# The first loads of an attention and MoE kernel: batch 0's first k as fp32 over SyncE's queue, its last fifth of v over the casting queue

## The chip, the cores and the metric

The kernel runs on one core of a Trainium2 chip. The metric is the device time of one execution in microseconds (us). TensorE is called PE in the profile, VectorE DVE, ScalarE ACT, GpSimd POOL and SyncE SP.

## The reference

Inputs are q, k and v of 8 batches, 8 heads, 576 positions and 64 dimensions, and two weight matrices, all fp32. Each head's output is the sum of two attentions. The first works on means over 4 neighbouring positions (144 of them) and is repeated 4 times; the second is local, over positions less than 4 apart. The heads are then put side by side (4608 tokens of 512 features), and a feed-forward block follows.

```
out_up    = repeat(attention(mean4(q), mean4(k), mean4(v)), 4)
out_local = attention(q, k, v) where |i - j| < 4
x   = (out_up + out_local), heads side by side      # 4608 x 512
h   = x @ w_in                                      # 4608 x 2048
out = (h * sigmoid(1.702 * h)) @ w_out              # 4608 x 512
```

## The kernel before

The tokens are worked through in 9 groups of 512. For each group `mm1` multiplies by w_in (L738) and `mm2` by w_out (L808), and the attention of the next batch is threaded between these matmuls. Only batch 0's attention has no matmuls to lie beside: it is the prologue, written out by hand from L847 to L938, and the order of the program's lines is the order on each engine (a manual schedule).

Data come in through two kinds of queue. A DMA issued by GpSimd casts fp32 to bf16 on its way (`load_1` for k and q, `load_vb` for values, `load_w_in`, `load_w_out`); one issued by SyncE or ScalarE moves bytes as they are. GpSimd's DMAs share eight semaphores in turn, so that each waits for the landing of the one issued eight before it.

The prologue's loads come in this order. At L847 `load_v` takes values chunk 4 of 5 (the last fifth) as fp32 in two halves of 128 KB, one over SyncE's queue and one over ScalarE's; ScalarE casts it into the bf16 tile vb at L865 (`prep_v`, recorded at L325). GpSimd issues k and q of heads 0 to 3, k and q of heads 4 to 7 (288 KB each as bf16), then chunks 0 to 3 of the values by `load_vb`, two halves of 64 KB each, then the first quarter of w_in. Between these loads GpSimd makes index tables (`iota_mask`, `iota_psel`), from which VectorE makes an identity, the mask bar `off` and the steps `rv` (`make_off`, `make_ident`, `make_psel`) and a bias (`make_bias`), and ScalarE a selection matrix psel (`end_psel`: seven Abs at L166, a Relu at L169, two Exp at L171).

VectorE transposes each k and q tile in 32x32 blocks (`prep_1`, L261) and sums groups of four positions (`reduce_qk`, L304). TensorE computes local scores (`scores`: the bar at L381, the products at L394) and, before them, throwaway matmuls from `warm` (L606). ScalarE exponentiates (L477, L483). `prep_vd_pe` (L362) sums four neighbouring values by matmuls with psel, first from chunks 0 and 1, then from 1, 2 and 3; its second call takes chunks 3 and 4. After the first call come the products with the values (`av_local0`, L499, all five chunks; `av_down0`, L513 and L522), a normalisation on VectorE (L541 to L549), the transposes back (L564, L575) and the first matmuls with w_in.

The persistent tile xT (four tiles of 128 x 4608 bf16) receives the attention's result, one batch after another; the last of the four gets batch 0's columns at L591, late in the prologue, and later batches' columns after that.

Of the kernel before, what the change touches and what calls it, by code (L numbers as in the profile page):

```python
# [8 lines left out]
FP32 = mybir.dt.float32  # L9
BF16 = mybir.dt.bfloat16  # L10
# [9 lines left out]
def kernel(  # L20
# [9 lines left out]
    nc = tc.nc  # L30
    B, H, S, D = q.shape
    SD = S // 4
    HP = H // 2
# [16 lines left out]
    ldp = ctx.enter_context(tc.tile_pool(name="loads", bufs=1))  # L50
# [10 lines left out]
    xT = [persist.tile([128, B * S], BF16, name=f"xT{i}") for i in range(HP)]  # L61
# [11 lines left out]
    def pm_tile():  # L73
        turn["m"] += 1
        return PM[turn["m"] % 2]
# [10 lines left out]
    di = consts.tile([128, 128], FP32, name="di")  # L86
    dr = consts.tile([128, 1], FP32, name="dr")
    bias = consts.tile([128, 4], FP32, name="bias")
# [5 lines left out]
    def iota_psel():  # L94
        for par in range(2):
            sl, c = halves[par], 2 * KSTART[par] - 512 * par - 3
            nc.gpsimd.iota(db[sl, 0:3], pattern=[[-72, 3]], base=c + 144,
                           channel_multiplier=-6, **it)
            nc.gpsimd.iota(db[sl, 3:7], pattern=[[72, 2], [-384, 2]], base=c + 228,
                           channel_multiplier=-6, **it)  # L100
# [8 lines left out]
    def fill():  # L109
        nc.vector.memset(wz, 0.0)  # L110
        nc.vector.memset(wf, 0.0)
        for t in kdT:
            nc.vector.memset(t[:, SD:160, :], 0.0)
        for t in vbs:
            nc.vector.memset(t[:, :, :, 64:65], 1.0)
        for t in vds:
            nc.vector.memset(t[:, :, :, 64:65], 4.0)
        for t in es:
            nc.vector.memset(t[:, :, 300:304], 1.0)
        for t in eds:  # L120
            nc.vector.memset(t[:, :, 432:480], 1.0)


    def make_off():
        nc.vector.tensor_tensor(out=dm, in0=dm, in1=dm, op=ALU.mult)
        nc.vector.tensor_single_scalar(out=dm, in_=dm, scalar=9.5, op=ALU.is_lt)
        nc.vector.tensor_scalar(
            out=off, in0=dm, scalar1=-1.0, scalar2=1e6, op0=ALU.add, op1=ALU.mult
        )
# [7 lines left out]
    def make_ident(di):  # L137
        nc.vector.tensor_single_scalar(out=id128, in_=di, scalar=0.0, op=ALU.is_equal)

    def make_bias():  # L140
        nc.vector.memset(bias[:, 3:4], -3.0)
        nc.vector.tensor_copy(out=bias[:, 0:2], in_=rv)
        nc.vector.tensor_scalar(
            out=bias[:, 0:2], in0=bias[:, 0:2], scalar1=-1.0, scalar2=400.0,
            op0=ALU.add, op1=ALU.mult,
        )

    rv = consts.tile([128, 2], FP32, name="rv")
    r2 = consts.tile([128, 2], FP32, name="r2")

    def make_psel():
        nc.vector.tensor_single_scalar(
            out=rv, in_=dr.to_broadcast([128, 2]), scalar=57.5, op=ALU.is_lt
        )
        nc.vector.tensor_single_scalar(
            out=r2, in_=dr.to_broadcast([128, 2]), scalar=65.5, op=ALU.is_gt
        )
        nc.vector.scalar_tensor_tensor(
            out=r2[:, 0:1], in0=dr, scalar=121.5, in1=r2[:, 0:1],
            op0=ALU.is_lt, op1=ALU.mult,  # L160
        )
        nc.vector.tensor_tensor(out=rv, in0=rv, in1=r2, op=ALU.add)

    def end_psel():
        for m in range(7):
            nc.scalar.activation(  # L166
                out=dp[:, m], in_=di[:, 0:64], func=AF.Abs, scale=8.0, bias=db[:, m : m + 1]
            )
        nc.scalar.activation(out=dp, in_=dp, func=AF.Relu, bias=bias[:, 3:4])  # L169
        for sl, c in ((slice(0, 1), 1), (slice(1, 7), 0)):  # L170
            nc.scalar.activation(  # L171
                out=psel[:, sl], in_=dp[:, sl],
                func=AF.Exp, scale=-400.0, bias=bias[:, c : c + 1],
            )


    qf, kf, vf = {}, {}, {}

    def load_1(name, src, store, b, qd):
        t = ldp.tile(  # L180
            [128, 1152], BF16, name=f"{name}b{qd}", tag=f"{name}b{qd}", bufs=2
        )
        nc.gpsimd.dma_start(  # L183
            out=t,
            in_=bass.AP(
                tensor=src.tensor, offset=src[b, 4 * qd].offset,
                ap=[[1152, 128], [1, 1152]],
            ),
        )
        store[b, qd] = t  # L190

    def load_qk(b, qd):
        load_1("k", k, kf, b, qd)
        load_1("q", q, qf, b, qd)

    def load_v(b, gate=None, chunks=range(5), queues=(nc.sync, nc.sync)):
        t = ldp.tile([128, 5, H, D], FP32, name="vf", tag="vf")
        vf[b] = t
        if gate is not None:
            gate(t[0:1, 0, 0, 0:1])  # L200
        for i in chunks:
            for par in range(2):
                queues[par].dma_start(
                    out=t[64 * par : 64 * par + 64, i],
                    in_=bass.AP(
                        tensor=v.tensor,
                        offset=v[b, 0].offset + (114 * i + KSTART[par]) * D,
                        ap=[[D, 64], [S * D, H], [1, D]],
                    ),
                )  # L210

    def load_vb(b, i):
        for par in range(2):
            nc.gpsimd.dma_start(
                out=vbs[b % 2][64 * par : 64 * par + 64, i, :, 0:D],
                in_=bass.AP(
                    tensor=v.tensor,
                    offset=v[b, 0].offset + (114 * i + KSTART[par]) * D,
                    ap=[[D, 64], [S * D, H], [1, D]],
                ),  # L220
            )
# [35 lines left out]
    def prep_1(name, b, qd):  # L257
        store, dst = {"k": (kf, kT), "q": (qf, qT)}[name]
        tt = work.tile([128, S, 2], BF16, name=f"{name}T{qd}", tag=f"{name}T{qd}", bufs=1)
        t32 = tt.rearrange("p t a -> p (t a)").bitcast(FP32)  # L260
        nc.vector.transpose(  # L261
            out=t32.rearrange("p (i c) -> p c i", c=18),
            in_=store[b, qd].bitcast(FP32).rearrange("p (c d) -> p c d", c=18),
        )
        dst[b, qd] = tt
# [57 lines left out]
    def prep_v(b, eng, i=slice(0, 5), h=slice(0, H)):  # L323
        cp = eng.copy if eng is nc.scalar else eng.tensor_copy
        cp(out=vbs[b % 2][:, i, h, 0:D], in_=vf[b][:, i, h])  # L325
# [277 lines left out]
    def warm(n, cols=512, t=None, z=wz):  # L603
        t = pm_tile() if t is None else t
        for _ in range(n):
            nc.tensor.matmul(  # L606
                t[:, 0:cols], lhsT=z[:, 0:128], rhs=z[:, 0:cols], start=True, stop=True
            )
# [233 lines left out]
    o, y, x = {}, {}, {}  # L842

    def after(src, eng):
        return lambda t: eng.tensor_copy(out=t, in_=src)

    load_v(0, chunks=[4], queues=(nc.sync, nc.scalar))  # L847
    nc.scalar.preload_act_table_set("exp_and_others")
    load_qk(0, 0)
    load_1("k", k, kf, 0, 1)  # L850
    iota_mask()
    load_1("q", q, qf, 0, 1)
    iota_psel()
    fill()
    for i in range(4):
        load_vb(0, i)
    load_w_in(0, 512)
    warm(3, z=wf)
    warm(5, 256)
    make_off()  # L860
    make_ident(di)
    make_psel()
    make_bias()
    end_psel()
    prep_v(0, nc.scalar, 4)  # L865
    prep_1("k", 0, 0)
    prep_1("q", 0, 0)
    sp = scores(0, 0, PA[0:2])
# [9 lines left out]
    for qd in range(NQ):  # L878
        load_qk(1, qd)
# [60 lines left out]
    for g in range(n_groups):  # L940
        b = g + 1
        if g == 0:
# [13 lines left out]
            for qd in range(NQ):  # L956
                load_qk(2, qd)
            nc.gpsimd.memset(v4[32:64], 0.0)
            for x, c in ((0, 1.0), (1, 4.0)):
                nc.vector.memset(ones[:, x, :], c)  # L960
            load_v(2, gate=after(w_out_bf[0:1, 14, 0:1], nc.gpsimd))
            load_v4(2)
        elif b == 2:
# [11 lines left out]
            load_qk(b + 1, 0)  # L975
            prep_vx(b)
            load_v(b + 1)
            prep_v4(b, nc.gpsimd, (0,))
            pool_qk(b, 1, "q")
# [77 lines left out]
```

## Time and profile before

| what | before |
|---|---|
| median of 3 runs | 309.1 us (309.04 to 310.23) |
| profiled execution | 308.58 us |
| its span, first to last instruction | 306.8 us |
| granted TensorE clock | 0.999 |
| busy: PE, DVE, ACT, POOL | 298.0, 187.1, 212.9, 178.9 us |
| share of the chain that ended last: PE, DMA, issue | 93%, 4%, 1% |

The span is the time between the first and last instruction of the profiled execution; its whole time holds 1.78 us more. Times in the trace count from the span's start. A busy PE is not one at its peak, since matmuls overlap. The chain that ended last is followed back from the last instruction, at each step to what released it, or to the instruction before it on its engine.

### The profile page before, as it was taken

The numbers are of one execution on the slowest core, as the hardware profiler recorded it, in microseconds if no ns is written. First come the engines' busy times: TensorE is split into PE (matmuls) and PEld (weight loads), VectorE is DVE, ScalarE is ACT, GpSimd is POOL, SyncE is SP. The second block draws the span as 40 slices with busy tenths as digits, with TensorE's granted clock in tenths as the row PEclk, the third lists the DMA queues.
The fourth block names the chain that finished last, engine by engine and source line by source line (L and its number), as shares of the span: only waits on it lengthen the run. The fifth ranks groups of instructions, "written<-read, shape, count | busy, mean of one in ns | idle before, by whom it ended". The sixth has DMA issues, their size and how long they took to land.

```text
span 306.8 us, 8494 instructions
## 1 busy us (share of the span) xinstructions
PE 298.0 (97%) x3551; PEld 147.8 (48%) x3551; DVE 187.1 (61%) x354; ACT 212.9 (69%) x351; POOL 178.9 (58%) x217
## 2 busy tenths in 40 slices
PE   7879999999999999999999999999999999999995
PEld 3455455444554455445544554455444544444444
DVE  6865523966999689886897689777975430000000
ACT  5545887867887788668966896689769876226511
POOL 8855792599698968976797669845983300000000
PEclk9999999999999999999999999999999999999999
DMA  7999999999899969826973598425101110010012
GB/s 147 152 203 209 173 132 213 177 221 215 177 230 188 188 133 226 219 46 113 232 211 66 88 218 232 84 77 150 72 0 37 36 71 0 34 71 34 0 68 71
DMA packets 64662, 40.01 MB, mean 130 GB/s; under 512 B 44656, under 2 KB 56048, under 8 KB 64624
## 3 DMA queue, kind: packets, MB, share of 16 engines
q0 software_dynamic: 18352, 14.81, 35.8%
q1 hardware_dynamic: 45600, 24.46, 32.3%
q8 instruction: 28, 0.46, 0.6%
q10 hardware_dynamic: 672, 0.20, 0.3%
q14 instruction: 10, 0.08, 0.1%
HBM read 44.83 MB, written 9.44 MB: 177 GB/s over the span
## 4 chain that ended last, share of the span: by engine, by line
PE 93%; DMA 4%; issue 1%; POOL 1%; DVE 0%; ACT 0%; POOLq 0%; DVEq 0%
PE pm L808 40%; PE pm L738 36%; PE pa L681 5%; PE pa L738 5%; DMA qb<-in_q_dram 2%; DMA vb<-in_v_dram 2%; PE pa L449 2%; PE pm L824 1%; PE pa L458 1%; PE pa L394 1%; PE pa L411 0%; POOL kb L183 0%; PE pa L513 0%; PE pa L362 0%; PE pa L499 0%
## 5 line engine op out<-in xcount | busy, mean ns | idle before, releaser
L808 PE MATMUL pm<-w_out_bf,gT 128*128 128x512 bf16 x560 | 126.2, 379 | 0.0
L738 PE MATMUL pm<-xT,w_in_bf 128*128 128x512 bf16 x512 | 119.2, 379 | 0.3 <-ACT xT L591 0.3
L749 ACT ACTIVATE gT<-pm 128x512 bf16<-128x512 f32 x128 | 76.3, 598 | 42.7 <-PE pm L738 42.7
L738 PEld LDWEIGHTS <-w_in_bf 128*128 128x128 bf16 x576 | 55.6, 98 | 67.2 <-issue 0.6
L808 PEld LDWEIGHTS <-gT 128*128 128x128 bf16 x560 | 52.9, 98 | 62.2 <-issue 0.4
L699 DVE TENSOR_TENSOR xT<-pa,r 128x300 bf16<-128x300 f32 (+3 forms) x112 | 28.0, 303 | 18.6 <-ACT r L694 17.8
L787 ACT ACTIVATE osb<-pm 128x512 f32<-128x512 f32 (+2 forms) x37 | 21.5, 580 | 24.1 <-PE pm L808 21.3
L708 POOL TENSOR_TENSOR xT<-xT,ydt 128x576 bf16<-128x576 bf16 x14 | 16.2, 1173 | 31.1 <-DVE xT L699 31.1
L789 DVE TENSOR_SCALAR osb<-pm 128x128 f32<-128x128 f32 x1 | 0.3, 292 | 55.5 <-ACT osb L787 55.5
L491 DVE TENSOR_TENSOR es<-es,mask 128x600 bf16<-128x600 bf16 x28 | 19.0, 708 | 21.2 <-ACT es L477 20.9
L693 ACT ACTIVATE r<-pa 128x504 f32<-128x504 f32 (+1 forms) x42 | 24.0, 571 | 8.4 <-PE pa L681 8.4
L694 ACT ACTIVATE r<-r 128x504 f32<-128x504 f32 (+1 forms) x42 | 25.9, 616 | 1.3
L339 POOL TENSOR_TENSOR v<-v 112x512 f32<-112x512 f32 x18 | 23.5, 1306 | 0.4
L277 DVE TENSOR_REDUCE kT<-kT 32x576 bf16<-32x576 bf16 x22 | 17.5, 795 | 8.7 <-POOL odd L272 8.3
L261 DVE STREAM_TRANSPOSE kT<-kb 128x576 f32<-128x576 f32 x16 | 20.0, 1252 | 3.4 <-DMA kb<-in_k_dram 3.1
L477 ACT ACTIVATE es<-pa 128x600 bf16<-128x600 f32 x32 | 19.7, 668 | 3.4 <-PE pa L394 3.2
L261 DVE STREAM_TRANSPOSE qT<-qb 128x576 f32<-128x576 f32 x16 | 19.8, 1238 | 0.7 <-DMA qb<-in_q_dram 0.3
L738 PE MATMUL pa<-xT,w_in_bf 128*128 128x512 bf16 x64 | 20.0, 379 | 0.0
L315 POOL TENSOR_TENSOR pq<-qT 128x576 f32<-128x576 bf16 x14 | 16.0, 1145 | 6.8 <-DVE qT L277 6.6
L277 DVE TENSOR_REDUCE kT<-odd 32x576 bf16<-32x576 bf16 x22 | 17.5, 795 | 0.7
L277 DVE TENSOR_REDUCE qT<-qT 32x576 bf16<-32x576 bf16 x22 | 17.5, 795 | 0.7
L277 DVE TENSOR_REDUCE qT<-odd 32x576 bf16<-32x576 bf16 x22 | 17.4, 791 | 0.7
(107 smaller groups left out, 344.2 us busy)
## 6 DMA issues: line engine op xcount, KB each, us to landing
out_dram<-osb SPq DMA_DIRECT2D x35, 256.0 KB, 3.2
vf<-in_v_dram SPq DMA_DIRECT2D x61, 128.0 KB, 4.3
v<-in_v_dram SPq DMA_DIRECT2D x72, 96.0 KB, 4.2
kb<-in_k_dram POOLq DMA_DIRECT2D x16, 288.0 KB, 7.1
qb<-in_q_dram POOLq DMA_DIRECT2D x16, 288.0 KB, 9.4
w_in_bf<-in_moe_w_in_dram POOLq DMA_DIRECT2D x4, 512.0 KB, 7.5
w_out_bf<-in_moe_w_out_dram POOLq DMA_DIRECT2D x3, 512.0 KB, 15.6
vb<-in_v_dram POOLq DMA_DIRECT2D x18, 64.0 KB, 6.3
```

The source lines that it names most:

```text
L261: nc.vector.transpose(out=t32.rearrange("p (i c) -> p c i", c=18), in_=store[b, qd].bitcast(FP32).rearrange("p (c d) -> p c d", c=18),)
L277: nc.vector.tensor_reduce(out=dst, in_=src[:, :, None], axis=mybir.AxisListType.X, op=ALU.add)
L339: eng.tensor_tensor(out=t1[0:112], in0=x[:, :, 0:2, :], in1=x[:, :, 2:4, :], op=ALU.add)
L477: nc.scalar.activation(out=es[2 * qd + u][:, :, 0:300], in_=sp[u][:, :, 0:300], func=AF.Exp, scale=inv_sqrt_d,)
L491: nc.vector.tensor_tensor(out=ev, in0=ev, in1=mask, op=ALU.mult)
L693: nc.scalar.activation(out=r, in_=den, func=AF.Ln)
L694: nc.scalar.activation(out=r, in_=r, func=AF.Exp, scale=-1.0)
L699: nc.vector.tensor_tensor(out=sub(x[u], t0 + at, (114, n), (1, c)), in0=sub(src, c0, (60, n), (1, c)), in1=sub(rc, c0, (60, n), (1, c)), o ...
L738: nc.tensor.matmul(acc, lhsT=w_in_bf[:, dmc, ffc * 128 : (ffc + 1) * 128], rhs=xT[dmc][:, g * TG : g * TG + TG], start=(dmc == 0), stop=(d ...
L749: nc.scalar.activation(out=gT[:, ffc, :], in_=acc, func=AF.Silu, scale=GELU_SCALE)
L787: eng.activation(out=osb, in_=ap, func=AF.Copy, scale=1.0 / GELU_SCALE)
L808: nc.tensor.matmul(ops[t], lhsT=gT[:, ffc, t * 128 : (t + 1) * 128], rhs=w_out_bf[:, ffc, :], start=(ffc % run == 0), stop=(ffc % run == r ...
```

## The change

The first k (batch 0, heads 0 to 3) is no longer loaded by GpSimd. SyncE issues it first of all as fp32 (128 x 1152), into the last xT tile, which holds nothing at that time; ScalarE casts its first half of columns and VectorE its second into the bf16 tile kb0. Values chunk 4 is no longer loaded as fp32 and cast by ScalarE; GpSimd loads it in two casting halves, ahead of chunks 0 to 3. The three operations of `make_bias` move from VectorE to GpSimd, where they stand between chunk 4 and chunk 0; `make_off`, `make_ident` and `make_psel` keep their order on VectorE, with the cast of k behind them. Of the throwaway matmuls, five of 256 columns become four of 128.

```diff
--- before.py
+++ after.py
@@ -138,9 +138,9 @@
         nc.vector.tensor_single_scalar(out=id128, in_=di, scalar=0.0, op=ALU.is_equal)
 
     def make_bias():
-        nc.vector.memset(bias[:, 3:4], -3.0)
-        nc.vector.tensor_copy(out=bias[:, 0:2], in_=rv)
-        nc.vector.tensor_scalar(
+        nc.gpsimd.memset(bias[:, 3:4], -3.0)
+        nc.gpsimd.tensor_copy(out=bias[:, 0:2], in_=rv)
+        nc.gpsimd.tensor_scalar(
             out=bias[:, 0:2], in0=bias[:, 0:2], scalar1=-1.0, scalar2=400.0,
             op0=ALU.add, op1=ALU.mult,
         )
@@ -189,18 +189,32 @@
         )
         store[b, qd] = t
 
+    def load_k0():
+        t = xT[HP - 1].bitcast(FP32)[:, 0:1152]
+        nc.sync.dma_start(
+            out=t,
+            in_=bass.AP(tensor=k.tensor, offset=k[0, 0].offset, ap=[[1152, 128], [1, 1152]]),
+        )
+        return t
+
+    def cast_k0(x):
+        t = ldp.tile([128, 1152], BF16, name="kb0", tag="kb0", bufs=2)
+        nc.vector.tensor_copy(out=t[:, 576:1152], in_=x[:, 576:1152])
+        nc.scalar.copy(out=t[:, 0:576], in_=x[:, 0:576])
+        kf[0, 0] = t
+
     def load_qk(b, qd):
         load_1("k", k, kf, b, qd)
         load_1("q", q, qf, b, qd)
 
-    def load_v(b, gate=None, chunks=range(5), queues=(nc.sync, nc.sync)):
+    def load_v(b, gate=None):
         t = ldp.tile([128, 5, H, D], FP32, name="vf", tag="vf")
         vf[b] = t
         if gate is not None:
             gate(t[0:1, 0, 0, 0:1])
-        for i in chunks:
+        for i in range(5):
             for par in range(2):
-                queues[par].dma_start(
+                nc.sync.dma_start(
                     out=t[64 * par : 64 * par + 64, i],
                     in_=bass.AP(
                         tensor=v.tensor,
@@ -844,25 +858,26 @@
     def after(src, eng):
         return lambda t: eng.tensor_copy(out=t, in_=src)
 
-    load_v(0, chunks=[4], queues=(nc.sync, nc.scalar))
+    k0 = load_k0()
     nc.scalar.preload_act_table_set("exp_and_others")
-    load_qk(0, 0)
+    load_1("q", q, qf, 0, 0)
     load_1("k", k, kf, 0, 1)
     iota_mask()
     load_1("q", q, qf, 0, 1)
     iota_psel()
     fill()
+    load_vb(0, 4)
+    make_off()
+    make_ident(di)
+    make_psel()
+    make_bias()
+    cast_k0(k0)
     for i in range(4):
         load_vb(0, i)
     load_w_in(0, 512)
     warm(3, z=wf)
-    warm(5, 256)
-    make_off()
-    make_ident(di)
-    make_psel()
-    make_bias()
+    warm(4, 128)
     end_psel()
-    prep_v(0, nc.scalar, 4)
     prep_1("k", 0, 0)
     prep_1("q", 0, 0)
     sp = scores(0, 0, PA[0:2])
```

## The prediction

> **What bounds the kernel now.** The page comes first: TensorE is busy 97% of 306.8 us and the chain that ended last is 93% PE, so a change at the front pays only by the time at which TensorE's dense stretch begins. I therefore read the chain of waits for the first 25 us (start, length, what):
>
> ```profile
> 2.47 0.53 POOL kb L183
> ...
> 3.87 6.09 DMA qb<-in_q_dram
> 9.96 0.28 issue
> 10.24 5.79 DMA vb<-in_v_dram
> 16.04 0.04 issue
> 16.08 0.30 PE pm L362 x2
> ...
> 20.53 1.22 issue
> ```
>
> The reader should see that no engine sets the first 16 us. GpSimd's queue does: its fourth load, q of heads 4 to 7 (q1), lands at 9.96, and its last values transfer, chunk 3's second half, is issued at 10.24 and lands at 16.03. From 16.08 the PE chain runs to the end with one hole, 1.22 us at 20.53.
>
> Next, the time line round the two places where TensorE meets these loads (start, length, engine, line; in brackets the idle time before and its releaser):
>
> ```profile
> 5.55 1.26 DVE L261 STREAM_TRANSPOSE kT<-kb 128x576 f32<-128x576 f32 x1 [0.25 <-DMA kb<-in_k_dram]
> 7.12 1.26 DVE L261 STREAM_TRANSPOSE qT<-qb 128x576 f32<-128x576 f32 x1 [0.31 <-DMA qb<-in_q_dram]
> 8.23 1.29 DVE L304 TENSOR_REDUCE kdT<-kT 128x288 bf16<-128x1152 bf16 x1
> ...
> 14.51 0.75 PE L362 MATMUL pm<-vb,psel 128*64 128x256 bf16 x8
> 16.08 0.30 PE L362 MATMUL pm<-vb,psel 128*64 128x256 bf16 x2 [0.82 <-DMA vb<-in_v_dram]
> ```
>
> VectorE works without a hole from 7.12 to 14.15, and what it feeds brings TensorE to L362 at 14.51. TensorE has done all it can there at 14.51 + 0.75 = 15.26 and idles 0.82 us for chunk 3. So the path through k, q, VectorE and the scores has 0.82 us of slack; values have none.
>
> Last, the DMA view by windows: the first 10 us (queue, packets, MB, share of 16 engines), then windows round single issues (KB, us from issue to landing), and 11 to 13 us:
>
> ```profile
> q1 hardware_dynamic: 528, 0.13, 5.8%
> q10 hardware_dynamic: 528, 0.13, 5.8%
> ...
> kb<-in_k_dram POOLq DMA_DIRECT2D x1, 288.0 KB, 4.3
> ...
> vb<-in_v_dram POOLq DMA_DIRECT2D x1, 64.0 KB, 6.0
> ...
> vb<-in_v_dram POOLq DMA_DIRECT2D x1, 64.0 KB, 5.7
> ...
> vb<-in_v_dram POOLq DMA_DIRECT2D x1, 64.0 KB, 6.6
> ...
> q8 instruction: 1, 0.02, 5.5%
> ```
>
> The vb rows are the first, fifth and sixth transfer. Issues start 0.69 us apart from 4.96, so these land at 10.96, 13.42 and 15.01: a pace of (13.42 - 10.96)/4 = 0.61 us each, then one step of 1.59. In that step one engine fetches 16 KB of instructions (5.5% of 16 engines times 2 us is 1.76 us on one), and a transfer has landed when its slowest engine is done. The lag of about 1 us stays until 16.03.
>
> **The change, part by part.**
>
> *Out of the queues.* The two hardware halves of chunk 4 leave: 5.8% of 10 us is 0.58 us of all engines each, 1.16 together. k's casting load leaves GpSimd: k1 lands at 2.44 + 6.1 = 8.54 and q1 at 9.96, so such a load is worth 1.43 us. Sum out: 2.59 us.
>
> *In: k as fp32 over SyncE.* Late in the run two fp32 stores of 256 KB take 7.0% of 20 us, 0.70 us each, so 576 KB take 1.58 us. It cannot be free, since it reads the same bytes as the casting load (1.43 at least), and twice that (2.86) would be the price of writing twice as much. I take 1.58, the nearest row. Hence q1 lands at 9.96 - 2.59 + 1.58 = 8.95.
>
> *In: chunk 4 as two casting transfers ahead of chunks 0 to 3.* At the pace of 0.61 that is 1.22 us. Lower bound: between 9.5 and 11 us the engines read 1210 small packets per us, so 512 take 0.42 us, 0.85 for two. Upper bound: the mean over the eight, (16.03 - 9.96)/8 = 0.76, so 1.52. I take 0.61, the pace at which transfers in fact land. Chunk 3 then lands at 16.03 - 1.01 + 1.22 = 16.24, 0.2 us **later**; the bounds give -0.16 and +0.51. The instruction fetch stays in this stretch, because it goes with TensorE's position in its code, which loses one warm-up matmul.
>
> *GpSimd's order.* One issue (0.69) fewer stands ahead of the values, so the first starts near 4.3. After the second come the three bias operations. GpSimd's smallest rows take 0.10 to 0.16 us (memset, iota), its 128x288 addition 0.67: 0.3 to 2.0 us for three, 0.5 taken, as the tiles are 1 or 2 columns wide. They wait for VectorE's rv, ready at 4.89 now and earlier after. Behind them queue eight values issues and the first w_in. The last issue starts at 4.3 + 9 x 0.69 + 0.5 = 11.0 instead of 10.24. With 4.3 us (the first k's row, almost alone) to 5.8 (the values' median) from issue to landing it lands between 15.3 and 16.8: the transfers, not the issue, still set 16.24. The w_in issue slips from 11.22 to about 11.9; it landed 6.5 us after its issue and is first read at 23.16, so nothing waits.
>
> *Casting k.* SyncE issues at 0.74. Its v half took 3.9 us to land; 1.0 more of transfer, partly beside q0, gives 4.9 (3.6 with the 2.0 us of the late stores, 5.6 at worst). ScalarE's half costs 0.65 (a 128x512 cast is 0.61). VectorE's 128x576 cast lies between 0.3 (its 128x128 cast takes 0.31) and 1.0 (that row and the 128x60 one, 0.21, extended); 0.65 taken. k's transpose starts at 5.6 against 5.55, and q's, whose data land near 6.0, at 6.9 against 7.12. VectorE's stretch moves by -0.2 us, inside the slack: nothing at the end. Without that cover it would cost its own shift, from 0.82 us on. The Trainium skill ("SBUF — State Buffer", Who interferes with whom) speaks against this cast: a two-port VectorE copy and GpSimd fully block one another, whoever comes first, and descriptors are written by GpSimd. No row shows it: the values issues keep 0.69 beside VectorE's transposes. By it the sum would be 0.3 to 1.0 us later at one issue or at the cast.
>
> *Hidden edits.* ScalarE drops the chunk 4 cast (0.61) and the DMA issue (0.72), and starts its seven Abs about 0.6 later; psel is done near 9.0, before the scores that it exponentiates next (9.32) and long before L362. Four short warm-ups for five leave TensorE idle some 0.6 us longer before 8.43; the granted clock is 1.00 in every stretch, also in 20 to 22 us, where PE is busy 0.78 of 2.00. Three bias operations leave VectorE (0.4 us), ahead of k's arrival.
>
> **Sum.** 306.8 + 0.2 = 307.0 us of span. The profiled execution took 308.58, 1.78 around the span, so 308.8; the median of the runs is 309.1, 0.5 above it, and I give the time on that scale: 309.3.
>
> **The rivals.**
>
> *Values come early.* If the two extra transfers cost 0.85 and the instruction fetch holds nothing up, chunk 3 lands at 16.03 - 0.95 - 0.16 = 14.9. Then VectorE's path decides: TensorE is ready at 15.1 to 15.26, a gain of 0.8, 308.3. For: reads did run at 0.42 early on. Against: landings never did. A gain over 1.55 needs the hole at 20.53 to close too (308.3 - 1.22 = 307.1). That hole follows a 16 KB fetch; the Trainium skill ("Runtime: NRT & Kernel Launch", Instruction fetch mechanics) calls such fetches mostly hidden, which the 1.22 us contradict, and the change does not touch it.
>
> *Slower: GpSimd's issue becomes the bound.* If the bias operations take 2.0 us, or the cast blocks an issue for 1.0, the last values issue starts at 12.0 to 13.5; with 5.8 us to landing chunk 3 comes at 17.8 to 19.3, 1.8 to 3.3 late: 310.9 to 312.4. It passes the forecast from an issue at 10.5 and costs 0.5% from 11.8. For: ten issues in a row with work between them. Against: rows of 0.10 to 0.16 for small operations, and the eighth transfer's 5.79 held a 1 us lag.
>
> *The early k is not early.* If k is cast only at 6.4, VectorE's stretch slips 0.6, still inside the slack: same time.
>
> **How the numbers follow.** Forecast, with the harmless late k, 0.71; values early 0.17, of which 0.05 with the hole closed; GpSimd as bound 0.12, of which 0.07 beyond 0.5%. About 0.5% (1.55 us) is what a measurement of this kernel can tell from no change. So faster 0.05, same 0.88, slower 0.07. The range takes in the early values and the first part of the slow rival: 308.2 to 310.5.
>
> **What would show it.** After: q1's transpose near 10.3, but still a wait for vb ahead of L362's last two matmuls, ending near 16.2; values issues from 4.3 to 11.7; VectorE's k cast at 4.9 to 5.6. I am wrong if L362 is released before 15.3 or after 17, if the hole at 20.53 changes by over half a microsecond, or if the granted clock falls below 1.00 before 16 us.

## The result, and the profile after

The changed kernel takes 311.05 us (median of 20 runs, 309.50 to 316.79) where the kernel before, beside it, takes 308.97 (20 runs, 307.52 to 312.74): the ratio is 1.0057, with an interval of 1.0031 to 1.0084. Two more measurements of the same kernel gave 1.0083 (1.0057 to 1.0108) and 1.0065 (1.0034 to 1.0097). It is slower by 0.6 to 0.8%, some 2 us; the forecast was 309.3 us, no change, with a range of 308.2 to 310.5. (The ratios leave out the few executions in a slower state, so they can differ a little from the quotient of the medians, and e18's profile, taken in one of these, is not read.) The profiled execution took 311.88 us, its span 309.8 against 306.8, so 2.08 us of it lie outside the span, against 1.78 before. The medians over the runs show the same (2.10 us in the changed kernel, some 1.8 in the kernel before): about 0.3 of the 2 us are lost outside the span, and no run here shows to what.

The first view is again the time line at the front (start, length, engine, line, operation, and in brackets the idle time before and its releaser), here of the changed kernel, VectorE and then TensorE:

```profile
4.29 0.46 DVE L202 CAST kb<-xT 128x576 bf16<-128x576 f32 x1
4.99 1.26 DVE L275 STREAM_TRANSPOSE kT<-kb 128x576 f32<-128x576 f32 x1 [0.24 <-ACT kb L203]
8.44 1.26 DVE L275 STREAM_TRANSPOSE qT<-qb 128x576 f32<-128x576 f32 x1 [2.18 <-DMA qb<-in_q_dram]
...
17.23 0.30 PE L376 MATMUL pm<-vb,psel 128*64 128x256 bf16 x2 [0.68 <-DMA vb<-in_v_dram]
```

k came as early as it was meant to: its transpose starts at 4.99 instead of 5.55. But q, issued 0.7 us earlier than before, was late: VectorE sat idle 2.18 us for it, and its first transpose starts at 8.44 instead of 7.12. The last pair of L376's matmuls (L362 before) starts at 17.23 instead of 16.08.

That is 1.15 us, and yet it is not the loss. These are the first matmuls with w_in, before and then after, from TensorE's time line:

```profile
23.18 0.59 PE L738 MATMUL pm<-xT,w_in_bf 128*128 128x512 bf16 x2
```

```profile
22.93 0.38 PE L752 MATMUL pm<-xT,w_in_bf 128*128 128x512 bf16 x1
```

The changed kernel is 0.25 us ahead there: the hole of 1.22 us at 20.53 is gone in this execution. That is its luck: e1 and e16, the same kernel again, have 0.54 and 0.39 us of it. It falls back later. The waits of TensorE in the changed kernel (line, releaser: us in total, times, longest) have a row that the kernel before does not have at all:

```profile
PE pm L822 <- DMA w_out_bf<-in_moe_w_out_dram: 2.3, 2, 1.5
```

and TensorE's time line has these two waits at 40 and 52 us:

```profile
41.21 2.10 PE L822 MATMUL pm<-w_out_bf,gT 128*128 128x512 bf16 x9 [0.82 <-DMA w_out_bf<-in_moe_w_out_dram]
...
54.02 0.59 PE L822 MATMUL pm<-w_out_bf,gT 128*128 128x512 bf16 x2 [1.49 <-DMA w_out_bf<-in_moe_w_out_dram]
54.54 0.35 PE L695 MATMUL pa<-es,ones 64*64 64x300 bf16 x6
```

The last row stood at 51.63 before:

```profile
51.63 0.35 PE L681 MATMUL pa<-es,ones 64*64 64x300 bf16 x6
```

So the change is 2.91 us behind at this point, and 3.0 at the end of the span. Where the weights' lateness comes from is told by the chain that ended last, followed back from there (start, length, what):

```profile
3.34 8.53 DMA qb<-in_q_dram
11.86 0.28 issue
12.15 2.03 POOL vb L228 x3
14.18 0.78 POOL w_in_bf L251
...
18.34 11.48 DMA w_in_bf<-in_moe_w_in_dram
...
30.10 13.01 DMA vb<-in_v_dram
...
45.63 8.35 DMA w_out_bf<-in_moe_w_out_dram
54.02 0.59 PE pm L822 x2
```

This is one line of GpSimd's DMAs, from q at 3.34 to w_out at 53.98. Since each waits for the landing of the one issued eight before it, a delay at the head is handed on. Issue by issue, the last three values come behind the landing of q1 at 11.86 (before, only the last one did, and q1 landed at 9.96); w_in is issued at 14.15 (before 11.22), its last three loads at 16.82 (13.89), the last three of w_out as below, before and then after in GpSimd's time line, and the very last lands at 53.98 (48.58):

```profile
39.21 2.23 POOL L246 DMA_DIRECT2D w_out_bf<-in_moe_w_out_dram  x3
```

```profile
44.16 2.19 POOL L260 DMA_DIRECT2D w_out_bf<-in_moe_w_out_dram  x3
```

The chain grows from 2.9 us late to 5.0 on its way, and TensorE comes for this weight 1.49 us before 54.02, at 52.53.

### The profile page after: what moved, and what is told of

Read it like the earlier page. It is cut to its first block, busy times and chain, and to the rows that moved or that the text cites. A ratio compares the mean times of both kernels' runs of the same rounds, so it can differ in the third digit from the quotient of the medians.

```text
span 309.8 us, 8448 instructions
## 1 busy us (share of the span) xinstructions
PE 292.6 (94%) x3508; PEld 147.2 (48%) x3550; DVE 187.3 (60%) x352; ACT 213.0 (69%) x351; POOL 180.1 (58%) x221
## 4 chain that ended last, share of the span: by engine, by line
PE 80%; DMA 13%; POOL 3%; issue 2%; DVE 0%; ACT 0%; POOLq 0%
PE pm L822 36%; PE pm L752 34%; PE pa L695 5%; DMA vb<-in_v_dram 4%; DMA w_in_bf<-in_moe_w_in_dram 4%; DMA qb<-in_q_dram 3%; DMA w_out_bf<-in_moe_w_out_dram 3%; PE pa L752 2%; PE pa L463 2%; PE pm L838 1%; POOL vb L228 1%; PE pa L472 1%; POOL w_in_bf L251 1%; POOL pq L329 0%; POOL w_out_bf L260 0%
## 5 line engine op out<-in xcount | busy, mean ns | idle before, releaser
L822 PE MATMUL pm<-w_out_bf,gT 128*128 128x512 bf16 x536 | 121.6, 379 | 5.8 <-issue 3.3
L228 POOL DMA_DIRECT2D vb<-in_v_dram x20 | 13.7, 690 | 10.2 <-DMA w_in_bf<-in_moe_w_in_dram 3.7
```

The source lines that it names most:

```text
L822: nc.tensor.matmul(ops[t], lhsT=gT[:, ffc, t * 128 : (t + 1) * 128], rhs=w_out_bf[:, ffc, :], start=(ffc % run == 0), stop=(ffc % run == r ...
```

## The experiments

Theory **E** (end of the chain): GpSimd's queue has more ahead of the weights, w_out comes late, and TensorE waits for it at 40 to 52 us. **A**: the fp32 load of k disturbs q's casting load behind it, and with it everything that follows on that queue. Against them stood **F** (the front: L376 starts later, that is all), **C** (VectorE's copy of k holds up GpSimd's descriptors) and **D** (a chance of the first measurement). In e2 and e3, **B** lays the loss on chunk 4's pair and the longer issue on GpSimd, and E is what became of it. Ratios are to the kernel before, run on the same chip, with the 95% interval; "q0" is q of heads 0 to 3, and its landing is that on its last DMA engine (7.10 in the kernel before, 8.41 in the changed one). One profile gives such a landing to about 1 us only: e8 and e17 load batch 0 as the kernel before does, and there q0 landed at 7.49 and 8.01, and q1 at 10.4 and 10.9 instead of 9.96.

### The change again, and its halves

**e1**, the changed kernel unedited.

> The changed kernel once more. Theory A (the fp32 load of the first k disturbs the casting load that starts while it runs): q of heads 0 to 3 lands again after 7.5 us with its 16 engines spread over more than 1 us, and the kernel is about 1.8 us slower. Theory D (chance of one profiled execution): q lands near 6.0 as forecast, and the 1.8 us come from elsewhere, the two more values transfers and what GpSimd issues behind them.

311.16 us, 1.0083 (1.0057 to 1.0108). q0 landed at 8.45, on its first engine at 5.28. TensorE waited 1.15 us for w_out at 52.88. D falls, and q's lag is no accident of one execution: in all eight profiles that have the early k in rows of 4608 bytes and chunk 4 as casting transfers, q0 landed at 7.54 to 8.45.

**e2**, the early k alone. From the kernel before:

```
+    k0 = load_k0()
     load_v(0, chunks=[4], queues=(nc.sync, nc.scalar))
-    load_qk(0, 0)
+    load_1("q", q, qf, 0, 0)
...
     make_bias()
+    cast_k0(k0)
```

> The kernel before with one part of the change: the first k comes as fp32 over SyncE's queue ahead of all and is cast by ScalarE and VectorE; chunk 4 stays on the hardware queues, the bias on VectorE. Theory A: q of heads 0 to 3 lands late (after 7.5 us) and the kernel is 0.5 to 2 us slower than before. Theory B (the two casting transfers of chunk 4 and the longer issue on GpSimd cost the time): q lands near 6.5, the time is that of before or up to 1 us less, since one issue fewer stands ahead of the values.

308.69 us, 0.9996 (0.9969 to 1.0023). q0 landed at 7.63: the landing that A gave, with the time that B gave. In time the early k by itself costs nothing and brings nothing, but its profile shows a gain and a loss. TensorE reached the first w_in matmul at 21.28, 1.90 us earlier than before, and then waited 0.90 and 0.53 us for w_out, whose last load landed at 51.13 (48.58 before).

**e3**, chunk 4 alone. From the kernel before:

```
-    load_v(0, chunks=[4], queues=(nc.sync, nc.scalar))
...
     fill()
+    load_vb(0, 4)
...
-    prep_v(0, nc.scalar, 4)
```

> The kernel before with the other part: chunk 4 comes as two casting transfers ahead of chunks 0 to 3; the first k stays a casting load, the bias on VectorE. Theory A: the first four loads land as before (q of heads 4 to 7 near 9.5, since 1.16 us of hardware transfers are gone), chunk 3 lands about 0.3 us later than before, the time within 0.5 us of before. Theory B: chunk 3 and the first w_in come 1.4 us later on GpSimd, w_out late by as much, and the kernel is 1.5 to 2 us slower.

309.73 us, 1.0042 (1.0016 to 1.0067). q0 landed at 6.78, so nothing disturbed it; still w_in's second load was issued at 15.82 instead of 13.89, w_out landed at 51.65 and TensorE waited 0.72 us for it at 51.69. By the middle values the two casting transfers carry half of the loss or more without any help from k; 0.42%, some 1.3 us, lies between A's bound of 0.5 and B's 1.5 to 2.

### Who disturbs q, and who pays

**e4**, k cast by ScalarE alone. From the changed kernel:

```
-        nc.vector.tensor_copy(out=t[:, 576:1152], in_=x[:, 576:1152])
-        nc.scalar.copy(out=t[:, 0:576], in_=x[:, 0:576])
+        nc.scalar.copy(out=t, in_=x)
```

> The changed kernel with the whole first k cast by ScalarE, VectorE's copy left out. Theory C (VectorE's copy keeps GpSimd from writing descriptors): the casting loads land without spread, q of heads 4 to 7 near 9, and the kernel is over 1 us faster than the changed one. Theory A: the loads land as late as in the changed kernel; VectorE waits for q in any case, so the later k (its cast takes 0.6 us longer) costs nothing and the time is that of the changed kernel.

310.82 us, 1.0064 (1.0043 to 1.0086), the same as the changed kernel. q0 landed at 7.54, the earliest of the eight. C is not the cause of the loss.

**e5**, the changed kernel with one load less further back: batch 1's chunk 0 isn't loaded but set to zero, so batch 1's result lacks it.

```
+        nc.vector.memset(vbs[1][:, 0, :, 0:64], 0.0)     (in fill, at the start)
...
-            load_vb(1, 0)
```

> The changed kernel, with the two casting transfers of batch 1's values chunk 0 left out (VectorE fills that chunk with zeros at the start), so batch 1's result lacks them. Theory E (the lost time is TensorE's wait for the last quarter of w_out near 52 us, the end of GpSimd's chain of loads, each held up by the landing of the one eight before it): that wait (1.49 us in the changed kernel) closes, w_out's last load lands over 1.2 us earlier, and the kernel is 1 to 2 us faster than the changed one. Theory F (the front, up to the first dense matmuls near 24 us, loses the time): nothing before 24 us changes, so the time stays within 0.5 us of the changed kernel's.

309.45 us, 1.0012 (0.9983 to 1.0040), although q0 landed at 8.19 as in the changed kernel. The waits of TensorE have no w_out row any more:

```profile
PE pa L409 <- DVE qT L276: 1.4, 1, 1.4
PE pm L377 <- DMA vb<-in_v_dram: 0.7, 2, 0.5
```

The front is as late as it was (the last pair of L377's matmuls starts at 17.09, against 17.23), and most of the loss is gone. F falls; E stands.

**e6 to e8**, batch 1's chunks 3 and 4 taken off GpSimd's queue and brought over SyncE's as fp32, then cast by VectorE: in the changed kernel (e6), in e2 (e7), and in the kernel before (e8).

```
             load_vb(1, 2)
-            load_vb(1, 3)
-            load_vb(1, 4)
+            # chunks 3 and 4: fp32 over nc.sync, copied by nc.vector
```

> The changed kernel with batch 1's values chunks 3 and 4 as fp32 over SyncE's queue, released by VectorE when w_in's third quarter has landed and cast by VectorE, instead of four casting transfers on GpSimd: the same bytes, off GpSimd's chain. Theory E: w_out's last load is issued 2 to 3 us earlier, the wait near 52 us closes, and the kernel is 1 to 2 us faster than the changed one, near the time before. Theory F: the time stays within 0.5 us of the changed kernel's.

> The same two chunks over SyncE's queue, in the kernel that has of the change only the first k over SyncE's queue (the time of before, with waits of 0.90 and 0.53 us for w_out near 50 us). Theory E: those waits close and it is 1 to 1.4 us faster than before, 307.5. Theory F: the time of before.

> The same two chunks over SyncE's queue, in the kernel before, where TensorE waits for no w_out load. Theory E: nothing to close, so within 0.5 us of before. Theory F: also the time of before; it tells the worth of these chunks by themselves from that of the wait.

Measured: 311.82 us, 1.0093 (1.0057 to 1.0129); 309.93, 1.0020 (0.9988 to 1.0052); 309.26, 1.0009 (0.9986 to 1.0032). E had hoped for a gain in e6 and e7, and missed. In e6 w_out landed at 51.09 and the wait near 52 us was gone, but TensorE waited 0.70 us for w_out at 41.12, and then for batch 1's values, as its time line shows:

```profile
46.89 0.64 PE L391 MATMUL pa<-vb,psel 128*64 128x256 bf16 x8 [0.86 <-DMA vb<-in_v_dram]
```

The matmuls of this row begin with chunk 2, which GpSimd still loads. It landed at 46.84 (44.91 in the changed kernel, 40.74 before); the chunks that were moved had landed by 43.77. That their fp32 bytes, now ahead of chunk 2, made it late is likely and not shown. So these three say nothing against E, but they do not measure it either: here the repair moved the wait to another load.

### The other halves, and the packets

**e9**, bias back on VectorE and the warm-up as before (`warm(5, 256)`); **e10**, k as a casting load in front of q again; **e12**, chunk 4 behind chunks 0 to 3. From the changed kernel:

```
# e9
-        nc.gpsimd.memset(bias[:, 3:4], -3.0)     (and the two behind it)
+        nc.vector.memset(bias[:, 3:4], -3.0)
# e10
-    k0 = load_k0()
+    load_1("k", k, kf, 0, 0)
-    cast_k0(k0)
# e12
-    load_vb(0, 4)
     for i in range(4):
         load_vb(0, i)
+    load_vb(0, 4)
```

> The changed kernel with the bias operations back on VectorE and the warm-up matmuls as before (5 of 256 columns), so that only the early fp32 k and the two extra casting transfers are left of the change. If these two carry the loss through GpSimd's DMA chain: 310.6 to 311.2 us (0.5 to 0.7% above before), with TensorE waiting over 1 us for w_out near 52 us. If the bias operations ahead of the values' issues (0.5 us on GpSimd) carry it: 309.3 to 309.8.

> The changed kernel with batch 0's first k as a casting load again, in front of q on GpSimd's queue; the two extra casting transfers and the bias operations on GpSimd stay. If the fp32 load's disturbance of q is part of the loss: q's first quarter is on all engines within 1 us, and the time is 309.7 to 310.2 us, w_out waited for by 0.7 us or less. If the two extra casting transfers and GpSimd's 0.5 us are all of it: 310.8 to 311.3.

> The changed kernel with chunk 4's two casting transfers issued after chunks 0 to 3 instead of ahead of them. The number of GpSimd's DMAs ahead of w_in and w_out is the same. If the loss comes from these coming late (the chain of issues): 310.6 to 311.3 us, w_out waited for near 52 us by over 0.7 us, although chunk 3 lands 1 us earlier than in the changed kernel. If the landing of chunk 3 at the end of the prologue carries it: 309.5 to 310.1.

Measured: e9 310.14 us, 1.0056 (1.0033 to 1.0080); e10 310.83, 1.0053 (1.0032 to 1.0075), with q0 landing at 6.78; e12 310.70, 1.0058 (1.0038 to 1.0079). In all three w_out landed at 51.5 to 52.5 and was waited for, by 1.0, 0.7 and 0.8 us. e9's time lies between the two ranges given for it, its ratio in the first one's. The bias operations cost nothing that shows, and the place of the two transfers in the queue does not matter. e10 missed A's own expectation of 309.7 to 310.2: with the pair in the queue, q's lag adds less than these intervals resolve.

**e11, e13, e14**: the early k in smaller packets. The fp32 load moves one row of a partition, 4608 bytes, in a packet: in the changed kernel's first 4 us the profile counts 144 packets with 0.59 MB on SyncE's queue, 128 of them such rows and 16 under 512 bytes. Laid out in four pieces with gaps between, it moves 1152 (e11, and e13 its repeat), in eight pieces 576 (e14); the result is the same.

```
-        t = xT[HP - 1].bitcast(FP32)[:, 0:1152]
+        t = xT[HP - 1].bitcast(FP32)[:, 0:1184].rearrange("p (a c) -> p a c", a=4)[:, :, 0:288]
...
-            in_=bass.AP(..., ap=[[1152, 128], [1, 1152]]),
+            in_=bass.AP(..., ap=[[1152, 128], [288, 4], [1, 288]]),
```

> The changed kernel with the fp32 k in packets of 1152 bytes in place of 4608 (the destination is four pieces of 288 elements, 8 elements apart); the casts read the pieces, the result is the same. If the large packets, standing in front of q's casting packets on the same engines, are what spreads q's landing: q's first quarter on its last engine before 7.2 us in place of 8.4, and the time 310.2 or less. If it is the fp32 load as such, or the casts of it: landing at 8.0 or later, 310.8 to 311.3.

> The kernel with the fp32 k in packets of 1152 bytes once more, beside the changed kernel on the same chip. If packet size is the cause: q's first quarter again on its last engine before 7.2 us, and 0.2 to 0.5% over before, the changed kernel beside it 0.55 to 0.85% over. If the first run was chance: q's last engine at 7.5 us or later and the same time as the changed kernel.

> The changed kernel with the fp32 k in packets of 576 bytes (eight pieces of 144 elements, 8 apart). By packet size: q's first quarter lands together (within 1.2 us over its engines), k itself 0.3 to 1 us later than with 1152 bytes since there are twice as many packets, and the time is within 0.2% of the run with 1152 bytes. If something else in the changed kernel spreads q: last engine near 8.4 us and 0.55% or more over before.

**e16**, the changed kernel unedited beside e13 and e14:

> The changed kernel unedited, as the measure of the others in this call: 310.5 to 311.2 us, q's first quarter on its last engine at 8.0 to 8.5 us, the last w_out load at 52 to 54 us and TensorE waiting over 0.7 us for it.

Measured: e11 309.40 us, 1.0029 (1.0001 to 1.0057); e13 310.23, 1.0033 (1.0004 to 1.0063); e14 309.35, 1.0025 (1.0000 to 1.0050); e16 310.40, 0.1 under its range, 1.0065 (1.0034 to 1.0097). q0 landed at 6.49, 6.60, 6.49, and 8.38 in e16; k itself came 1 to 1.5 us later (5.15, 5.25, 5.68 against 4.19). The DMA view of 4 to 8 us (packets, MB, rate; then the casting queue with the time of its packets as a share of 16 engines' time) of the kernel before, of e16 and of e13:

```profile
DMA packets 409, 0.84 MB, mean 209 GB/s; under 512 B 46, under 2 KB 46, under 8 KB 409
q0 software_dynamic: 409, 0.84, 111.6%
```

```profile
DMA packets 274, 0.57 MB, mean 143 GB/s; under 512 B 25, under 2 KB 25, under 8 KB 274
q0 software_dynamic: 274, 0.57, 96.7%
```

```profile
DMA packets 412, 0.76 MB, mean 190 GB/s; under 512 B 44, under 2 KB 121, under 8 KB 412
q0 software_dynamic: 322, 0.67, 97.8%
```

A casting packet takes 111.6% x 16 x 4 us / 409 = 0.175 us before, 96.7% x 64 / 274 = 0.226 in the changed kernel and 97.8% x 64 / 322 = 0.194 in e13. From 4 to 8 us the rate was 124 to 156 GB/s in the eight profiles with large packets and chunk 4 cast, 190 to 217 in the three with small packets, and 195 in e3 and e10, which have no fp32 load. So the loads beside and behind the large packets are slow, and with small ones they are not. As the small ones also land later, the packets' size and their time change together, and these runs do not part the two. It is not size alone: e2 and its twin e7 have the same large packets with the small v transfers behind them, and there the rate over all queues was 206 and 219 GB/s, a casting packet took 0.184 and 0.176 us, and q0 landed at 7.63 and 6.74. With small packets about half of the loss is left, by the middle values; each of the three intervals overlaps those of the changed kernel.

**e15**, the early k in packets of 1152 bytes, without the pair of casting transfers (chunk 4 as before, bias on VectorE).

> Batch 0's first k early in fp32 packets of 1152 bytes, and chunk 4 over SyncE's and ScalarE's queues as before (cast by ScalarE), bias on VectorE: the early k alone, without its large packets. If chunk 4's two casting transfers are what is left of the loss: 308.0 to 309.0 us, the same as before or up to 0.3% faster, no wait for w_out over 0.4 us. If the early k costs something of its own: 309.4 or more.

308.54 us, 0.9990 (0.9961 to 1.0020). This version beats the changed kernel, and is the same as the kernel before. So the half that is left goes with the pair, again by the middle values (e13's interval begins at 1.0004).

### The price of the pair alone

**e17, e18**: the kernel before with two spare casting transfers of 64 KB into a place that nothing reads, ahead of w_in's last three loads (e17), or ahead of the last three of w_out (e18). Batch 0's k, q and values stand ahead of both, and are loaded as before.

```
# e17
     reduce_qk(0, 1, "k")
+    load_spare()
     for c in range(1, 4):
         load_w_in(512 * c, 512)
# e18
             load_vb(1, 4)
+            load_spare()
             load_w_out(8)
```

> The kernel before with two spare casting transfers of 64 KB (chunk 4's values, into a place that nothing reads) on GpSimd's queue ahead of w_in's last three loads; everything ahead of them, and the prologue, stays. If the price is the weights behind them coming late: 309.5 to 310.2 us (0.25 to 0.45% over before), w_out's last load landing near 50.5 us in place of 48.6 and TensorE waiting 0.4 to 1.2 us for it, w_in not waited for. If the price is paid in the prologue's values instead: 308.7 to 309.1, the same as before.

> The kernel before with the two spare transfers only ahead of the last three w_out loads (near 38 us). If the price of the pair is the end of the chain alone: again 309.5 to 310.2 us and w_out waited for between 48 and 52 us. If it comes from w_in and the first w_out loads as well: less, 308.8 to 309.4. If neither carries it: the same as before, 308.7.

Measured: e17 310.53 us, 1.0057 (1.0033 to 1.0081); e18 310.71, 1.0046 (1.0021 to 1.0071). GpSimd's time line of e17, and its TensorE at 51 us:

```profile
14.67 1.39 POOL L226 DMA_DIRECT2D xT<-in_v_dram  x2
16.04 2.29 POOL L248 DMA_DIRECT2D w_in_bf<-in_moe_w_in_dram  x3
```

```profile
51.34 0.59 PE L819 MATMUL pm<-w_out_bf,gT 128*128 128x512 bf16 x2 [0.50 <-DMA w_out_bf<-in_moe_w_out_dram]
```

Two spare transfers that nobody reads cost about what the whole change costs, whether they stand ahead of w_in or only ahead of w_out. That is E's price without any change to batch 0's loads. Both times lie above the 309.5 to 310.2 us that were expected, and TensorE's wait in e18 wasn't seen, since no profile of it is read. One caution: e17's profiled execution is the fastest of its 12 runs (309.18 of 309.18 to 311.89), so its wait of 0.50 us is a low sample of a loss of 1.6 us in the medians. And its w_in was issued at 12.00, not 11.22, already ahead of the spare transfers.

**The loss at w_out, profile by profile.** In the kernel before, the first w_in matmul is at 23.18, the first matmul with the last load of w_out at 51.11 and the L681 row shown above at 51.63. So TensorE takes 27.93 us from the first to the second and 28.45 to the third, and it waits for no w_out load on the way. The table counts in each profile from its own first w_in matmul (all in us):

| profile | first w_in matmul | 27.93 later | last w_out load lands | late by | time to the row, beyond 28.45 |
|---|---|---|---|---|---|
| before | 23.18 | 51.11 | 48.58 | not late | 0 |
| changed | 22.93 | 50.86 | 53.98 | 3.12 | 3.16 |
| e1 (changed) | 23.64 | 51.57 | 52.84 | 1.27 | 1.31 |
| e16 (changed) | 22.80 | 50.73 | 52.28 | 1.55 | 1.60 |
| e2 (k alone) | 21.28 | 49.21 | 51.13 | 1.92 | 1.96 |
| e3 (pair alone) | 22.46 | 50.39 | 51.65 | 1.26 | 1.31 |
| e5 (one load less) | 22.79 | 50.72 | 50.32 | not late | 0.00 |
| e15 (k in small packets, no pair) | 22.63 | 50.56 | 50.48 | not late | -0.01 |
| e17 (spare pair) | 22.52 | 50.45 | 51.30 | 0.85 | 0.89 |

What TensorE loses up to this row is the lateness of the last w_out load, to 0.05 us, and nothing where the load is in time. It also says why e2 has a late w_out and no loss: it had come 1.90 us earlier. In the changed kernel's first profile this is the whole loss of the span (3.0 us). In e1 and e16 it is not: their spans end 3.5 and 2.5 us behind, and more is lost after this row. In e16 TensorE waits once more at 111 us:

```profile
111.37 0.40 PE L472 MATMUL pa<-qdT,kdT 64*64 64x144 bf16 x12 [1.07 <-POOL qdT L333]
```

GpSimd, which makes that tile, had itself stood 3.80 us for a later load of values, until 91.87 (0.60 us in the changed kernel's first profile, none before). So loads behind w_out are late too; how often that costs time isn't measured.

**What stays open.** Why casting packets stay slow until 8.4 us when the large load had landed at 4.27, and why they do not with the v transfers behind it (e2, e7). What makes the 0.3 us outside the span, and what e1 loses behind 54 us. A version with the early k whose w_out loads come earlier than the values of batch 1 wasn't tried.

## Why the prediction was wrong, step by step

- **The end of the prologue and its slack: right as a reading, not what decides.** L376's last pair was still released by values, at 17.23 and not 16.24, which is past the bound of 17 that I had set. But TensorE reached the w_in matmuls no later than before, since the 1.22 us hole, which I had said the change does not touch, was gone in that execution. The prediction ended its account at the front: "a change at the front pays only by the time at which TensorE's dense stretch begins". This is the sentence that failed. It follows TensorE's instructions, and left out that GpSimd's queue is one chain that runs from the front to 54 us. In its place: the last w_out load landed at 53.98 instead of 48.58, 3.12 us after TensorE's time for it, and that is the loss of the span.
- **"q1 lands at 9.96 - 2.59 + 1.58 = 8.95": failed, measured 11.86.** Two parts. The loads taken out did not give back the 2.59 us: with chunk 4's halves gone and k still a casting load (e3, e10) q1 landed at 10.70 and 11.05, no earlier than the 9.96 to 10.9 of the profiles that have them, and in e11, with k's casting load gone too and small packets in, at 9.91. The fp32 load itself was sized about right (44.2% of the first 4 us, 1.77 us against 1.58). The other part goes with the large packets: q1 landed at 11.04 to 11.86 in the eight profiles that have them and a cast chunk 4, at 9.91 to 10.40 in the three with small ones. No row of the trace before had shown that, since its hardware loads moved packets of 256 bytes.
- **Chunk 4 as two casting transfers, 0.61 each: the engines' time was right, the place was wrong.** The ten transfers land from 12.21 to 17.18, 0.55 us each; what the two cost is their place in the queue. Before, one values issue stood between q1's landing and w_in, now three (2.03 us). In e17 and e18 two transfers further back cost as much.
- **GpSimd's order: right in its arithmetic, wrong in its input and in its end.** With the measured q1, 11.86 + 0.29 + 2.03 = 14.18 is the w_in issue that the trace has (14.15); with e11's, 9.91 + 0.29 + 2.04 = 12.24 (12.20). The bias operations took 0.10 + 0.18 + 0.19 us, the 0.5 that was forecast. But "it landed 6.5 us after its issue and is first read at 23.16, so nothing waits" looked at the next transfer alone. w_in was indeed never waited for; w_out, at the end of the same chain, was.
- **Casting k: right in its result, not in its working.** The load landed at 4.27 (4.9 forecast, though its own terms, 0.74 + 3.9 + 1.0, make 5.64), VectorE took 0.46 us and ScalarE 0.67 (0.65 each forecast), and the transpose began at 4.99 (5.6): that it came early enough owes something to luck. What followed failed: q0, forecast near 6.0, landed at 8.41, and VectorE's stretch moved by +1.32 us where -0.2 was forecast, more than its slack of 0.82. The Trainium skill ("SBUF — State Buffer", Who interferes with whom) has a VectorE copy in a two-port mode and GpSimd block one another. The trace is in line with that: the iota beside the cast took 0.46 us, and 0.14 without the VectorE copy (e4); that the cast ran in such a mode no row shows. The next values issue started at 4.43 with the copy and without it, so nothing behind moved, and the time is the same (e4).
- **Hidden edits: right.** e9 puts back the bias and the warm-up and is not faster by more than the intervals.
- **The rivals.** "GpSimd's issue becomes the bound", at 0.12, came nearest: it had the last values issue late and a time of 310.9 to 312.4. That the time agrees is luck. Its mechanism was another one (bias operations or the cast, not q1's landing), it priced the landing of chunk 3 and not that of the weights, and its chance of 0.07 beyond 0.5% was far too small for a queue of which the profile shows that each issue waits for the eighth before.

## What to carry to other kernels

Before a transfer is added to a queue, follow that queue to its end, not to the next reader: find the last load on it that is read soon after it lands (here w_out, landing at 48.6 and read at 51.1), since that is the slack that the new transfer has to fit in. Where a step is hidden at its own place, ask what is issued behind it and where its delay comes out. And a load moved to another queue still shares the engines: look whether its packets are of a size that the trace has already seen beside the others.

## What the runs showed of the hardware

- Beside and behind an fp32 load in packets of 4608 bytes over a hardware queue, casting loads were slow until some 4 us after it had landed: 124 to 156 GB/s from 4 to 8 us in eight profiles, against 190 to 217 with packets of 1152 and 576 bytes and 209 in the kernel before. The Trainium skill ("DMA: Bandwidth & Descriptors", SWDGE vs HWDGE vs iDMA) has a packet preferably no larger than 4096 bytes, and engines that change between queues only at packet boundaries; it says so of the packets that GpSimd builds, and this load is SyncE's. The runs agree as far as 4608 did harm and 1152 and 576 did not; they do not show where the boundary lies, nor does that rule say why the harm outlasts the load, or why it was absent in e2 and e7 with the same 4608.
- Two casting transfers of 64 KB that nothing reads cost 0.57% (e17, 0.33 to 0.81) and 0.46% (e18, 0.21 to 0.71) on a core whose TensorE is busy 97% of the time.
- The hole of 1.22 us at 20.53, seen before, came back at 20.29 in e12 (1.16 us) and was absent in the changed kernel. In the nine profiles that have it (0.28 to 1.22 us) it ends 1.2 to 1.6 us after a fetch of 16 KB of instructions has landed (20.38 and 21.75 in the kernel before). So it depends on when the code fetch gets through and isn't a fixed cost.
